# Six-layer cross network on one core: first group half turned by DMA, another order of the last jobs, the last layer regrouped

## The chip, the cores and the metric

The kernel runs on one core of a Trainium2 chip. The metric is the device time of one execution in microseconds (us): the median of 13 runs is 494.12 (491.48 to 496.78). Lower is better.

The engines have names as in the profile: PE is the matrix engine, PEld its weight loads, DVE the vector engine, ACT the scalar engine, POOL the one for odd work, SP the one that here only issues DMAs. ACT issues some DMAs too; on either engine the issue is an instruction of its queue, taken in order with the rest.

## The reference

A cross network of six layers over 16384 rows of 416 features in bf16:

```
x = x0                                   # [16384, 416]
for l in range(6):
    proj = einsum('bd,de->be', x, ws[l]) + bs[l]
    x = x0 * proj + x
return x
```

Each layer is one 416 x 416 matrix product, a bias, a product with the input x0 and a sum with the layer's own input.

## The kernel before

**Tiling.** The rows are cut into 8 groups of 2048 (`GC`), each into 4 chunks of 512 (`CH`, index j). Inside the kernel x is kept turned: features on the 128 partitions, rows along the free axis. The 416 features are three tiles of 128 (index t or i) and a rest of 32; the rest of all four chunks is packed on one 128-partition tile (`x3`, 32 partitions a chunk). Group g and layer l make a job (g, l); a job is three output tiles and a tail (the 32 last outputs). `full` (L399) issues the twelve 128x128 matmuls of a tile, `rows32` (L412) the four that take the 32 rest rows, `tails` (L422) the tails of several jobs. `evacuate` (L347) empties a tile: ACT adds the bias on the way out of PSUM (L364), DVE multiplies by x0 (L373) and adds x (L378). A tail goes the same way (L391, L393, L395).

**Order.** `order` (L217) lists the 48 jobs by hand along diagonals, so that two jobs of one group have others between them, but for the first two and the last two. `items` turns it into tiles and batches of tails; tiles go in pairs, the first with the rest rows last (FR), the second with the rest rows first (RF), singles are F1. At the end one tile of job (6, 5) is put between two of (7, 4) (L565). `Program` keeps one queue for each engine in program order and works out the semaphore waits from what each instruction reads and writes; DVE's adds are held back behind the next product (`hold`, `release`). An instruction that waits holds everything behind it on its engine.

**Front.** Group 0 comes in natural layout, a chunk at a time (`load_nat`, L459, on SP). PE turns it: 28 small matmuls on an identity first (L480), then for each chunk twelve transposes (L494) and four for the rest columns (L499), emptied by ACT (L504, twice a chunk) and DVE (L507, L510). The biases are turned likewise (L639 to L648). `load_w3` (L282) issues four small loads of a layer's last 32 weight rows; layers 0 and 1 go on ACT's queue. Every other group but the last is turned by DMA (`load_group`, L294): three transposes of 2048 x 128, one of the last 128 columns into `Tb`, and from there four copies of 32 partitions, each waiting for `Tb` (L305).

**End.** When a group's last layer is done, `output` (L531) turns it back by DMA into `ost` on SP's queue: tile 0, tile 1, four small transposes of the rest (L543), tile 2 (L535), then, after all have landed, one store (L550). Group 7's last layer is computed with rows on the partitions instead (from L759): `nat_full` (L716) and `nat_rows` (L727, L732) for each of four row sets kk, `to_rows` turns x by PE (L691, L698) and ACT and DVE copy it out (L708, L711), `nat_mul` (L744, L746; the very last one directly from PSUM, L741), `nat_add` (L751), `nat_store` (L756).

Of the kernel before, what the change touches and what calls it, by code (L numbers as in the profile page):

```python
# [3 lines left out]
P = 128  # L4
CH = 512
T32 = 32
# [192 lines left out]
def bass_standalone__cross_network_dcn__recsys_kernel(  # L199
# [19 lines left out]
             (2, 4), (3, 3), (4, 1), (5, 0)]  # L219
    order += [(NG - 1 - g, L - 1 - l) for g, l in reversed(order)]  # L220
    assert len(set(order)) == NG * L
    cuts = [1, 2, 3, 4, 4, 4, 4, 4, 4, 4, 4, 4, 3, 2]
# [14 lines left out]
    bs_sb = nc.alloc_sbuf_tensor("bs_sb", [P, D], BF16)  # L237
    brow = nc.alloc_sbuf_tensor("brow", [P, D], BF16)
    ones = nc.alloc_sbuf_tensor("ones", [P, P], BF16)
    x0s = [nc.alloc_sbuf_tensor(f"x0_{s}", [P, XW + CH], BF16) for s in range(NX0)]  # L240
# [105 lines left out]

    def evacuate(g, l, i, banks, js, step):  # L347

# [6 lines left out]
        src, stok = x_src(g, l)  # L355
        so = xset[(g, l + 1)]
        a = js[0]
        while a <= js[-1]:
# [100 lines left out]
    def load_nat(j, k0, k1):  # L459
        add("sp", lambda h: h.dma_start(x0n[:, j, k0:k1, :], perm(g0, j)[:, k0:k1, :]),  # L460
            writes=[("nat", j, k) for k in range(k0, k1)], lane=f"nat{j}{k0}", batch=0)

    add("act", lambda h: h.dma_start(bs_sb[0:L, :], bs[:, :]), writes=["bs_sb"], lane="bs", batch=0)
    load_nat(0, 0, 2)
    load_nat(0, 2, KK)
    load_wm(0, "sp")
    load_w3(0, "act")
    make_wbd(0)
    for j in range(1, NJ):
        load_nat(j, 0, KK)  # L470
    load_wm(1, "sp")
    load_w3(1, "act")
    load_group(1)
# [4 lines left out]

    for _ in range(28):
        add("pe", lambda h: h.matmul(psum[:, 7 * CH:7 * CH + P], ident[:, :], ident[:, :], start=True, stop=True),  # L480
            reads=["ident"], writes=[("ps", 7)])

    def psum_t(b):
        return psum[:, b * CH:(b + 1) * CH].bitcast(BF16)

    def transposed_chunk(j):
        ba, bb = (0, 1) if j % 2 == 0 else (2, 3)
        s = slot(0)
        for t in range(NT + 1):
            b, o = (ba, t * CH) if t < 2 else (bb, (t - 2) * CH)  # L490
            for k in range(KK):
                c = slice(o + k * P, o + (k + 1) * P)
                if t < NT:
                    add("pe", lambda h, t=t, k=k, b=b, c=c: h.transpose(  # L494
                        psum_t(b)[:, c], x0n[:, j, k, t * P:(t + 1) * P], ident[:, :]),
                        reads=[("nat", j, k), x0_tok(nat, 0, 0), "ident"], writes=[("ps", b)])
                else:
                    q = slice(j * T32, (j + 1) * T32)
                    add("pe", lambda h, k=k, b=b, c=c, q=q: h.matmul(  # L499
                        psum_t(b)[q, c], x0n[:, j, k, NT * P:D], ident[:, :], is_transpose=True,  # L500
                        tile_position=(0, j * T32)),
                        reads=[("nat", j, k), x0_tok(nat, 0, 0), "ident"], writes=[("ps", b)])
        for t in range(2):
            add("act", lambda h, t=t: h.activation(  # L504
                x0s[s][:, cols(t, j)], psum_t(ba)[:, t * CH:(t + 1) * CH], ACT_F.Copy),
                reads=[("ps", ba)], writes=[x0_tok(s, t, j)])
        add("dve", lambda h: h.tensor_copy(x0s[s][:, cols(2, j)], psum_t(bb)[:, 0:CH]),  # L507
            reads=[("ps", bb)], writes=[x0_tok(s, 2, j)])
        q = slice(j * T32, (j + 1) * T32)
        add("dve", lambda h: h.tensor_copy(x0s[s][q, XW:XW + CH], psum_t(bb)[q, CH:2 * CH]),  # L510
            reads=[("ps", bb)], writes=[("x03q", s, j)])


# [17 lines left out]
    def output(g):  # L531
# [9 lines left out]
        for j in range(NJ):  # L541
# [5 lines left out]
        rows = out[g * GC:(g + 1) * GC, :]  # L547
        pat = "(j p k) f -> p j k f" if g == 0 else "(j k p) f -> p j k f"
        kw = dict(j=NJ, k=KK)
        add("sp", lambda h: h.dma_start(  # L550
            rows.rearrange(pat, **kw), ost[:, :, :].rearrange("p (j k) f -> p j k f", j=NJ)),
            reads=[("ost", t) for t in range(NT)] + [("ost", NT, j) for j in range(NJ)],
            writes=[("out", g)], lane="out", batch=g)
        free_x.append(s)
# [3 lines left out]
    where = {(b[min(1, len(b) - 1)], 0): b for b in batches[:-1]}  # L558
    where[((LAST - 1, L - 1), 1)] = batches[-1]
    for jb in order[:-1]:  # L560
        for i in range(NT):
            items.append(("tile", jb, i))
            if (jb, i) in where:
                items.append(("tails", where[(jb, i)]))
    late = items.index(("tile", (LAST - 1, L - 1), NT - 1))  # L565
    items.insert(len(items) - 2, items.pop(late))

# [29 lines left out]

    fine_after = {(0, 0), (LAST, L - 2)}
    k = 0
    open_rf = None  # L600
    tiles_done = {}

    def finish_tile(g, l):
        tiles_done[(g, l)] = tiles_done.get((g, l), 0) + 1
        if tiles_done[(g, l)] == NT:
            done_with(g, l)
# [15 lines left out]

    first_tile = True
    for n, it in enumerate(items):
# [4 lines left out]
        if (g, l) not in started:  # L629
            start_job(g, l)  # L630
        fine = (g, l) in fine_after
        step = 1 if fine and i == NT - 1 else 2
        if mode[n] in ("FR", "F1"):
            if first_tile:
                first_tile = False
                transposed_chunk(0)
                bt = 7
                for t in range(NT):
                    add("pe", lambda h, t=t: h.transpose(  # L639
                        psum_t(bt)[:, t * 8:t * 8 + L], bs_sb[0:L, t * P:(t + 1) * P], ident[0:L, 0:L]),  # L640
                        reads=["bs_sb", "ident"], writes=[("ps", bt)])
                for j in range(NJ):
                    q = slice(j * T32, (j + 1) * T32)
                    add("pe", lambda h, j=j, q=q: h.matmul(
                        psum_t(bt)[q, NT * 8:NT * 8 + L], bs_sb[0:L, NT * P:D], ident[0:L, 0:L],
                        is_transpose=True, tile_position=(0, j * T32)),
                        reads=["bs_sb", "ident"], writes=[("ps", bt)])
                add("act", lambda h: h.activation(  # L648
                    bias[:, :, :], psum_t(bt)[:, 0:32].rearrange("p (t l) -> p t l", l=8)[:, :, 0:L], ACT_F.Copy),
                    reads=[("ps", bt)], writes=["bias"])  # L650
                banks = [4, 5, 6, 7]
                for j in range(1, NJ):
                    transposed_chunk(j)
                    full(g, l, i, banks, True, True, chunks=[j - 1])
                full(g, l, i, banks, True, True, chunks=[NJ - 1])
            else:
                banks = job_banks()
                full(g, l, i, banks, True, fine and i == NT - 1)
            rows32(g, l, i, banks, False)
            evacuate(g, l, i, banks, list(range(NJ)), step)  # L660
        else:
            banks = job_banks()
            rows32(g, l, i, banks, True)
            if step == 1:
                full(g, l, i, banks, False, True,
                     lambda j, g=g, l=l, i=i, banks=banks: evacuate(g, l, i, banks, [j], 1))
            else:
                full(g, l, i, banks, False, False)
                evacuate(g, l, i, banks, list(range(NJ)), step)
        finish_tile(g, l)  # L670


# [86 lines left out]
    bka, bkb = take(NJ), take(NJ)  # L759
    for j in range(NJ):  # L760
        nat_full(0, j, bka[j], True)
    nat_rows(0, bka, False)
    for j in range(NJ):
        nat_mul(0, j, bka[j])
    nat_rows(1, bkb, True)
    for j in range(NJ):
        nat_full(1, j, bkb[j], False)
        nat_mul(1, j, bkb[j])
    to_rows(0, bka)
    to_rows(1, bkb)  # L770
    nat_rows(2, bka, True)
    for kk in range(2):
        for j in range(NJ):
            nat_add(kk, j)
        nat_store(kk, 0, NJ, f"out7_{kk}")
    for j in range(NJ):
        nat_full(2, j, bka[j], False)
        nat_mul(2, j, bka[j])
        if j:
            nat_add(2, j - 1)  # L780
    nat_add(2, NJ - 1)
    nat_store(2, 0, NJ, "out7_2")
    nat_rows(3, bkb, True)
    for j in range(NJ):
        nat_full(3, j, bkb[j], False)
        nat_mul(3, j, bkb[j])
        if j:
            nat_add(3, j - 1)
        if j == 2:
            nat_store(3, 0, 2, "out7_3")  # L790
    nat_add(3, NJ - 1)
    nat_store(3, 2, NJ, "out7_4", "act")

# [29 lines left out]
```

## Time and profile before

| | us |
|---|---|
| median of 13 runs | 494.12 |
| the profiled execution | 491.52 |
| its span, first to last instruction | 489.7 |
| PE, DVE, ACT busy | 472.9, 405.7, 343.3 |
| DMA: 47.65 MB, mean | 97 GB/s |

The span is what the instructions cover; the 1.8 us to the execution's time lie around it. The page's second part cuts the span into 40 equal slices of 12.2 us, each a digit for the busy tenths of an engine. A line of a timeline gives start, length, engine, line of the kernel, operation, what is written and read, how many were merged, and in brackets how long the engine had been idle before it and what ended that. An engine's name with q behind it is its queue: a DMA issue or a wait, in which the engine does no work. The length of an issue is not that of the transfer; the landing is a separate event of the trace. A line of the view by stretches gives the stretch, its length, the busy time of PE, PEld, DVE, ACT and POOL, the granted clock of PE as a share, the DMA share and GB/s. Lengths of matmuls overlap; the distance from start to start tells the rate.

### The profile page before, as it was taken

How to read it: one execution, taken by the hardware profiler on the slowest of the kernel's cores; microseconds unless marked ns; L12 is line 12 of the kernel's file. 1: busy time of each engine (PE TensorE's matmuls, PEld its weight loads, DVE VectorE, ACT ScalarE, POOL GpSimd, SP SyncE). 2: the span in 40 equal slices, each digit the busy share in tenths (PEclk: the TensorE clock that was granted, in tenths of full speed). 3: DMA queues.
4: the chain of work that ended last, by engine and by line, in shares of the span. 5: the costliest groups of instructions: out<-in, count | busy, mean ns of one | idle time of the engine just before them, and what ended most of it. 6: DMA issues, size and time to landing. Idle time of an engine off the chain costs nothing.

```text
span 489.7 us, 8048 instructions
## 1 busy us (share of the span) xinstructions
PE 472.9 (97%) x3197; PEld 202.7 (41%) x3251; DVE 405.7 (83%) x710; ACT 343.3 (70%) x372; POOL 11.4 (2%) x37
## 2 busy tenths in 40 slices
PE   7999999999999999999999999999999999999985
PEld 6343444444444444444444444444444444344443
DVE  1778888888888888888888888888888888888877
ACT  3676777677677677767677767767767776677765
POOL 2022200000000000000000000000000000000000
PEclk9999999999999999999999999999999999999998
DMA  8795972000001387269316962570000236045656
GB/s 248 142 188 133 178 142 53 0 1 0 2 1 37 62 227 139 50 114 225 77 20 121 229 93 40 112 269 1 1 1 1 44 55 183 8 80 136 146 137 194
DMA packets 127689, 47.65 MB, mean 97 GB/s; under 512 B 107674, under 2 KB 126244, under 8 KB 127652
## 3 DMA queue, kind: packets, MB, share of 16 engines
q1 hardware_dynamic: 126984, 46.71, 42.9%
q8 instruction: 25, 0.41, 0.3%
q10 hardware_dynamic: 668, 0.43, 0.3%
q14 instruction: 12, 0.10, 0.1%
HBM read 5.97 MB, written 13.63 MB: 40 GB/s over the span
## 4 chain that ended last, share of the span: by engine, by line
PE 90%; DVE 4%; ACT 2%; issue 2%; DMA 1%; SPq 0%; DVEq 0%
PE ps L405 73%; PE ps L417 8%; PE ps L430 5%; ACT tw L364 2%; PE ps L435 2%; DMA x<-in_x_dram 1%; DVE x L378 1%; PE ps L716 1%; DVE x L751 1%; DVE tw L373 1%; PE ps L691 1%; PE ps L494 0%; DVE x L746 0%; ACT ts L391 0%; PE ps L499 0%
## 5 line engine op out<-in xcount | busy, mean ns | idle before, releaser
L364 ACT ACTIVATE tw<-ps,bias 128x1024 bf16<-128x1024 f32 (+1 forms) x296 | 300.6, 1070 | 129.8 <-PE ps L417 107.7
L405 PE MATMUL ps<-x,wm 128*128 128x512 bf16 x1638 | 372.6, 379 | 6.5 <-issue 3.7
L373 DVE TENSOR_TENSOR tw<-tw,x 128x1024 bf16<-128x1024 bf16 (+1 forms) x286 | 194.1, 683 | 68.4 <-ACT tw L364 68.1
L405 PEld LDWEIGHTS ps<-x,wm 128*128 128x128 bf16 x1692 | 158.8, 98 | 215.7 <-issue 28.2
L378 DVE TENSOR_TENSOR x<-tw,x 128x1024 bf16<-128x1024 bf16 (+1 forms) x286 | 182.1, 678 | 0.0
L417 PE MATMUL ps<-x,w 32*128 32x512 bf16 x564 | 44.5, 380 | 0.3 <-DVE x L395 0.3
L430 PE MATMUL ps<-x,wm 128*32 128x512 bf16 x564 | 38.7, 380 | 0.0
L391 ACT ACTIVATE ts<-ps,bias 128x512 bf16<-128x512 f32 x47 | 28.7, 699 | 0.0
L417 PEld LDWEIGHTS ps<-x,w 32*128 32x128 bf16 x564 | 9.0, 92 | 33.5 <-issue 32.4
L430 PEld LDWEIGHTS ps<-x,wm 128*32 128x32 bf16 x564 | 13.8, 96 | 15.5 <-issue 3.2
L395 DVE TENSOR_TENSOR x<-ts,x 128x512 bf16<-128x512 bf16 x47 | 18.7, 422 | 0.0
L393 DVE TENSOR_TENSOR ts<-ts,x 128x512 bf16<-128x512 bf16 x47 | 18.7, 421 | 0.0
L435 PE MATMUL ps<-x,wbd 128*32 128x512 bf16 x188 | 18.3, 379 | 0.0
L716 PE MATMUL ps<-wm,x 128*128 128x416 bf16 x48 | 9.7, 343 | 1.7 <-DVE x L378 1.7
L291 POOL COPY wbd<-w 32x32 bf16<-32x32 bf16 x24 | 9.3, 386 | 39.8 <-DMA w<-in_ws_dram 38.6
L507 DVE COPY x<-ps 128x512 bf16<-128x512 bf16 x4 | 1.7, 424 | 10.1 <-PE ps L499 10.1
L744 ACT ACTIVATE x<-ps 128x416 bf16<-128x416 f32 x15 | 6.8, 536 | 3.1 <-PE ps L732 2.4
L716 PEld LDWEIGHTS ps<-wm,x 128*128 128x128 bf16 x48 | 4.9, 116 | 6.2 <-DVE x L378 2.8
L435 PEld LDWEIGHTS ps<-x,wbd 128*32 128x32 bf16 x188 | 5.0, 97 | 5.1
L746 DVE TENSOR_TENSOR x<-x,x 128x416 bf16<-128x416 bf16 x15 | 5.4, 373 | 1.9 <-ACT x L744 1.7
L504 ACT ACT_TABLE_LOAD x1 | 1.3, 1283 | 6.3 <-issue 6.3
L504 ACT ACTIVATE x<-ps 128x512 bf16<-128x512 bf16 x8 | 4.3, 602 | 1.2 <-PE ps L494 1.2
(32 smaller groups left out, 42.7 us busy)
## 6 DMA issues: line engine op xcount, KB each, us to landing
out_dram<-ost SPq DMA_DIRECT2D x7, 1664.0 KB, 7.4
x<-in_x_dram SPq DMA_DIRECT2D x7, 416.0 KB, 6.4
wm<-in_ws_dram SPq DMA_DIRECT2D x6, 312.0 KB, 3.4
out_dram<-x SPq DMA_DIRECT2D x3, 416.0 KB, 2.9
x<-Tb SPq DMA_DIRECT2D x28, 32.0 KB, 1.8
ost<-x SPq DMA_TRANSPOSE x49, 2.4
x<-in_x_dram SPq DMA_DIRECT2D x2, 208.0 KB, 2.7
w<-in_ws_dram SPq DMA_DIRECT2D x16, 26.0 KB, 2.2
```

The lines of the kernel that those rows point to most:

```text
L291: add("pool", lambda h, q=q: h.tensor_copy(wbd[l][q, q], w3[l][q, NT * P:D]), reads=[("w3", l, j)], writes=[("wbd", l)])
L364: add("act", lambda h, a=a, w=w, b0=b0: h.activation(tw[r][:, a * CH:(a + w) * CH], psum[:, b0 * CH:(b0 + w) * CH], ACT_F.Identity, bias=b ...
L373: add("dve", lambda h, a=a, e=e: h.tensor_tensor(tw[r][:, a * CH:e * CH], tw[r][:, a * CH:e * CH], x0s[s0][:, i * GC + a * CH:i * GC + e * ...
L378: add("dve", lambda h, a=a, e=e: h.tensor_tensor(xs[so][:, i * GC + a * CH:i * GC + e * CH], tw[r][:, a * CH:e * CH], src(i, a, e), ALU.ad ...
L391: add("act", lambda h: h.activation(ts[r][:, :], bank(b), ACT_F.Identity, bias=bias[:, 3, l:l + 1], scale=1.0), reads=[("ps", b), "bias"], ...
L393: add("dve", lambda h: h.tensor_tensor(ts[r][:, :], ts[r][:, :], x0s[s0][:, XW:XW + CH], ALU.mult), reads=[("ts", r)] + x03_toks(s0), writ ...
L395: add("dve", lambda h: h.tensor_tensor(x3s[so][:, :], ts[r][:, :], src, ALU.add), reads=[("ts", r)] + stok, writes=[("x3", so)], hold=True)
L405: add("pe", lambda h, t=t, j=j: h.matmul(bank(banks[j]), wm[l][:, t, ecols], src(t, j, j + 1), start=(first and t == 0), stop=(not first a ...
L417: add("pe", lambda h, q=q, j=j: h.matmul(bank(banks[j]), w3[l][q, ecols], src[q, :], start=first, stop=not first, tile_position=(j * T32, 0)),
L430: add("pe", lambda h, t=t, j=j, src=src, l=l, b=b: h.matmul(bank(b, j * T32, (j + 1) * T32), wm[l][:, t, NT * P:D], src(t, j, j + 1), star ...
L435: add("pe", lambda h, j=j, s3=s3, l=l, b=b: h.matmul(bank(b, j * T32, (j + 1) * T32), wbd[l][:, j * T32:(j + 1) * T32], s3, start=False, s ...
L716: add("pe", lambda h, t=t: h.matmul(bank(b, n=D), xcol(t, j, kk), wm[l][:, t, :], start=(first and t == 0), stop=(not first and t == NT - 1)),
```

## The change

- Of group 0 only chunks 0 and 1 are loaded in natural layout and turned by PE. Chunks 2 and 3 are turned by DMA: SP issues a transpose of 1024 rows into half of `Tb`, three more into x0, and ACT's queue gets the two copies from `Tb` to x0.
- ACT runs a small activation first (on a tile that DVE clears); layer 1's small weights are issued by SP; 14 small matmuls stand ahead of the transposes instead of 28; chunk 0 is turned in two halves.
- Job (0, 0) is written out (`first_job`): its tile 0 and 1 by chunks, half of tile 0 emptied by DVE alone (`vector` in `evacuate`), tile 2 chunk by chunk, the job's tail last.
- The last jobs run as (5,5), (7,3), (6,4), (7,4), (6,5), (7,5); no tile is moved among them, and the last tails stand after tile 0 of (7, 4).
- The last layer turns two row sets, computes one, turns the other two, computes three; products, adds and stores follow each row set; the last store holds one chunk instead of two.
- Group 0's store is two DMAs.

```diff
--- before.py
+++ after.py
@@ -218,6 +218,7 @@
              (0, 4), (1, 3), (2, 2), (3, 1), (0, 5), (1, 4), (2, 3), (3, 2), (4, 0), (1, 5),
              (2, 4), (3, 3), (4, 1), (5, 0)]
     order += [(NG - 1 - g, L - 1 - l) for g, l in reversed(order)]
+    order[-6:] = [(5, 5), (7, 3), (6, 4), (7, 4), (6, 5), (7, 5)]
     assert len(set(order)) == NG * L
     cuts = [1, 2, 3, 4, 4, 4, 4, 4, 4, 4, 4, 4, 3, 2]
     batches = []
@@ -236,6 +237,7 @@
     bias = nc.alloc_sbuf_tensor("bias", [P, 4, L], FP32)
     bs_sb = nc.alloc_sbuf_tensor("bs_sb", [P, D], BF16)
     brow = nc.alloc_sbuf_tensor("brow", [P, D], BF16)
+    warm = nc.alloc_sbuf_tensor("warm", [P, 8], FP32)
     ones = nc.alloc_sbuf_tensor("ones", [P, P], BF16)
     x0s = [nc.alloc_sbuf_tensor(f"x0_{s}", [P, XW + CH], BF16) for s in range(NX0)]
     xs = [nc.alloc_sbuf_tensor(f"x_{s}", [P, XW], BF16) for s in range(NXS)]
@@ -344,7 +346,7 @@
             if 4 < g + NX0 <= LAST:
                 load_group(g + NX0)
 
-    def evacuate(g, l, i, banks, js, step):
+    def evacuate(g, l, i, banks, js, step, vector=()):
 
         s0 = slot(g)
         r = tw_n[0] % NTW
@@ -354,6 +356,17 @@
             r = (tw_n[0] - 1) % NTW
         src, stok = x_src(g, l)
         so = xset[(g, l + 1)]
+        for a in vector:
+            o = slice(a * CH, (a + 1) * CH)
+            add("dve", lambda h, a=a, o=o: h.scalar_tensor_tensor(
+                out=tw[r][:, o], in0=bank(banks[a]), scalar=bias[:, i, l:l + 1],
+                in1=x0s[s0][:, i * GC + a * CH:i * GC + (a + 1) * CH], op0=ALU.add, op1=ALU.mult),
+                reads=[("ps", banks[a]), "bias", x0_tok(s0, i, a)], writes=[("tw", r, a)])
+        for a in vector:
+            o = slice(a * CH, (a + 1) * CH)
+            add("dve", lambda h, a=a, o=o: h.tensor_tensor(
+                xs[so][:, i * GC + a * CH:i * GC + (a + 1) * CH], tw[r][:, o], src(i, a, a + 1), ALU.add),
+                reads=[("tw", r, a), stok(i, a)], writes=[("x", so, i, a)])
         a = js[0]
         while a <= js[-1]:
             if step > 1 and a % 2 == 0 and a + 1 <= js[-1] and banks[a + 1] == banks[a] + 1:
@@ -460,23 +473,35 @@
         add("sp", lambda h: h.dma_start(x0n[:, j, k0:k1, :], perm(g0, j)[:, k0:k1, :]),
             writes=[("nat", j, k) for k in range(k0, k1)], lane=f"nat{j}{k0}", batch=0)
 
+    add("dve", lambda h: h.memset(warm[:, :], 0.0), writes=["warm"])
+    add("act", lambda h: h.activation(warm[:, :], warm[:, :], ACT_F.Identity, bias=0.0, scale=1.0),
+        reads=["warm"], writes=["warm"])
     add("act", lambda h: h.dma_start(bs_sb[0:L, :], bs[:, :]), writes=["bs_sb"], lane="bs", batch=0)
     load_nat(0, 0, 2)
     load_nat(0, 2, KK)
     load_wm(0, "sp")
+    load_nat(1, 0, KK)
     load_w3(0, "act")
     make_wbd(0)
-    for j in range(1, NJ):
-        load_nat(j, 0, KK)
+    half = slice(2 * CH, GC)
+    add("sp", lambda h: h.dma_start_transpose(Tb[:, half], g0[half, D - P:D]), writes=["Tb"], lane="Tb", batch=0)
+    for t in range(NT):
+        add("sp", lambda h, t=t: h.dma_start_transpose(
+            x0s[0][:, t * GC + 2 * CH:(t + 1) * GC], g0[half, t * P:(t + 1) * P]),
+            writes=[x0_tok(0, t, j) for j in (2, 3)], lane=f"x0_00{t}", batch=0)
+    for j in (2, 3):
+        q = slice(j * T32, (j + 1) * T32)
+        add("act", lambda h, q=q, j=j: h.dma_start(x0s[0][q, XW:XW + CH], Tb[P - T32:P, j * CH:(j + 1) * CH]),
+            reads=["Tb"], writes=[("x03q", 0, j)], lane="x03_00", batch=0)
     load_wm(1, "sp")
-    load_w3(1, "act")
+    load_w3(1, "sp")
     load_group(1)
     load_wm(2, "sp")
     load_w3(2, "sp")
     make_wbd(1)
     make_wbd(2)
 
-    for _ in range(28):
+    for _ in range(14):
         add("pe", lambda h: h.matmul(psum[:, 7 * CH:7 * CH + P], ident[:, :], ident[:, :], start=True, stop=True),
             reads=["ident"], writes=[("ps", 7)])
 
@@ -486,20 +511,22 @@
     def transposed_chunk(j):
         ba, bb = (0, 1) if j % 2 == 0 else (2, 3)
         s = slot(0)
-        for t in range(NT + 1):
+        seq = [(t, k) for t in range(NT) for k in range(KK)]
+        if j == 0:
+            seq = [(t, k) for k2 in (0, 2) for t in range(NT) for k in (k2, k2 + 1)]
+        for t, k in seq + [(NT, k) for k in range(KK)]:
             b, o = (ba, t * CH) if t < 2 else (bb, (t - 2) * CH)
...
+            c = slice(o + k * P, o + (k + 1) * P)
...
@@ -510,6 +537,41 @@
         add("dve", lambda h: h.tensor_copy(x0s[s][q, XW:XW + CH], psum_t(bb)[q, CH:2 * CH]),
             reads=[("ps", bb)], writes=[("x03q", s, j)])
 
+    def first_job():
+
+        g, l = 0, 0
+        start_job(g, l)
+        transposed_chunk(0)
...
+        ba, bb = [4, 5, 6, 7], [0, 1, 2, 3]
+        full(g, l, 0, ba, True, True, chunks=[0])
+        transposed_chunk(1)
+        full(g, l, 0, ba, True, True, chunks=[1])
+        full(g, l, 1, bb, True, True, chunks=[0, 1])
+        full(g, l, 0, ba, True, True, chunks=[2, 3])
+        rows32(g, l, 0, ba, False)
+        evacuate(g, l, 0, ba, [0, 1], 2, vector=[2, 3])
+        full(g, l, 1, bb, True, True, chunks=[2, 3])
+        rows32(g, l, 1, bb, False)
+        rows32(g, l, 2, ba, True)
+        evacuate(g, l, 1, bb, list(range(NJ)), 2)
+        full(g, l, 2, ba, False, True, lambda j: evacuate(g, l, 2, ba, [j], 1))
+        finish_tile(g, l, NT)
+        tails([(g, l)])
+
 
     def job_banks():
         return take(NJ)
@@ -545,25 +607,27 @@
                 reads=[("x3", s3)], writes=[("ost", NT, j)], lane="ot", batch=g)
         turn(2)
         rows = out[g * GC:(g + 1) * GC, :]
-        pat = "(j p k) f -> p j k f" if g == 0 else "(j k p) f -> p j k f"
-        kw = dict(j=NJ, k=KK)
-        add("sp", lambda h: h.dma_start(
-            rows.rearrange(pat, **kw), ost[:, :, :].rearrange("p (j k) f -> p j k f", j=NJ)),
-            reads=[("ost", t) for t in range(NT)] + [("ost", NT, j) for j in range(NJ)],
-            writes=[("out", g)], lane="out", batch=g)
+        o = ost[:, :, :].rearrange("p (j k) f -> p j k f", j=NJ)
+        parts = [("(j k p) f -> p j k f", 0, NJ)]
+        if g == 0:
+            parts = [("(j p k) f -> p j k f", 0, 2), ("(j k p) f -> p j k f", 2, NJ)]
+        for pat, j0, j1 in parts:
+            add("sp", lambda h, pat=pat, j0=j0, j1=j1: h.dma_start(
+                rows[j0 * CH:j1 * CH, :].rearrange(pat, j=j1 - j0, k=KK), o[:, j0:j1, :, :]),
+                reads=[("ost", t) for t in range(NT)] + [("ost", NT, j) for j in range(NJ)],
+                writes=[("out", g, j0)], lane="out", batch=g)
...
     items = []
     where = {(b[min(1, len(b) - 1)], 0): b for b in batches[:-1]}
-    where[((LAST - 1, L - 1), 1)] = batches[-1]
-    for jb in order[:-1]:
+    where[((LAST, L - 2), 0)] = batches[-1]
+    del where[((0, 0), 0)]
+    for jb in order[1:-1]:
         for i in range(NT):
             items.append(("tile", jb, i))
             if (jb, i) in where:
                 items.append(("tails", where[(jb, i)]))
-    late = items.index(("tile", (LAST - 1, L - 1), NT - 1))
-    items.insert(len(items) - 2, items.pop(late))
 
 
     single = 0
...
-    first_tile = True
+    first_job()
     for n, it in enumerate(items):
         if it[0] == "tails":
             tails(it[1])
@@ -628,45 +689,16 @@
         _, (g, l), i = it
...
         if mode[n] in ("FR", "F1"):
...
-                full(g, l, i, banks, True, fine and i == NT - 1)
+            banks = job_banks()
+            full(g, l, i, banks, True, False)
             rows32(g, l, i, banks, False)
-            evacuate(g, l, i, banks, list(range(NJ)), step)
+            evacuate(g, l, i, banks, list(range(NJ)), 2)
         else:
             banks = job_banks()
             rows32(g, l, i, banks, True)
-            if step == 1:
-                full(g, l, i, banks, False, True,
-                     lambda j, g=g, l=l, i=i, banks=banks: evacuate(g, l, i, banks, [j], 1))
-            else:
-                full(g, l, i, banks, False, False)
-                evacuate(g, l, i, banks, list(range(NJ)), step)
+            full(g, l, i, banks, False, False)
+            evacuate(g, l, i, banks, list(range(NJ)), 2)
         finish_tile(g, l)
 
 
@@ -757,39 +789,31 @@
             reads=[("on", j, kk) for j in range(j0, j1)], writes=[("out7", kk, j0)], lane=lane, batch=0)
 
     bka, bkb = take(NJ), take(NJ)
-    for j in range(NJ):
-        nat_full(0, j, bka[j], True)
-    nat_rows(0, bka, False)
-    for j in range(NJ):
-        nat_mul(0, j, bka[j])
-    nat_rows(1, bkb, True)
-    for j in range(NJ):
-        nat_full(1, j, bkb[j], False)
-        nat_mul(1, j, bkb[j])
+    last = KK - 1
+
+    def layer_rows(kk, bks):
+        nat_rows(kk, bks, True)
+        for j in range(NJ):
+            nat_full(kk, j, bks[j], False)
+            nat_mul(kk, j, bks[j])
+            if j:
+                nat_add(kk, j - 1)
+            if kk == last and j == 2:
+                nat_store(kk, 0, 2, "out7_3")
+            if kk == last and j == 3:
+                nat_store(kk, 2, 3, "out7_4")
+        nat_add(kk, NJ - 1)
+        if kk < last:
+            nat_store(kk, 0, NJ, f"out7_{kk}")
+        else:
+            nat_store(kk, NJ - 1, NJ, "out7_5", "act")
+
     to_rows(0, bka)
-    to_rows(1, bkb)
-    nat_rows(2, bka, True)
-    for kk in range(2):
-        for j in range(NJ):
-            nat_add(kk, j)
-        nat_store(kk, 0, NJ, f"out7_{kk}")
-    for j in range(NJ):
-        nat_full(2, j, bka[j], False)
-        nat_mul(2, j, bka[j])
-        if j:
-            nat_add(2, j - 1)
-    nat_add(2, NJ - 1)
-    nat_store(2, 0, NJ, "out7_2")
-    nat_rows(3, bkb, True)
-    for j in range(NJ):
-        nat_full(3, j, bkb[j], False)
-        nat_mul(3, j, bkb[j])
-        if j:
-            nat_add(3, j - 1)
-        if j == 2:
-            nat_store(3, 0, 2, "out7_3")
-    nat_add(3, NJ - 1)
-    nat_store(3, 2, NJ, "out7_4", "act")
+    layer_rows(0, bkb)
+    to_rows(1, bka)
+    layer_rows(1, bkb)
+    layer_rows(2, bka)
+    layer_rows(3, bkb)
 
     pr.emit()
 
```

## The prediction

> **What bounds the kernel now.** I read the page's busy row first, then the chain that ended last in order of time, then the timeline of the two ends, the SP queue among it.
>
> ```profile
> PE 472.9 (97%) x3197; PEld 202.7 (41%) x3251; DVE 405.7 (83%) x710; ACT 343.3 (70%) x372; POOL 11.4 (2%) x37
> PE   7999999999999999999999999999999999999985
> ```
>
> TensorE is busy 97% and in tenths of 9 from slice 2 to slice 38; only the first and the last two slices show room. The middle needs no further reading: what the change moves at either end comes through one for one. The front, in the timeline:
>
> ```profile
> 1.79 3.17 PE L480 MATMUL ps<-ident 128*128 128x128 bf16 x28 [1.79 <-POOL ident L449]
> 6.30 1.28 ACT L504 ACT_TABLE_LOAD   x1 [6.30 <-issue]
> 7.59 1.09 ACT L504 ACTIVATE x<-ps 128x512 bf16<-128x512 bf16 x2
> ...
> 16.81 2.35 SPq L301 DMA_TRANSPOSE Tb<-in_x_dram  x1
> 21.33 2.50 SPq L305 DMA_DIRECT2D x<-Tb  x4
> ...
> 24.06 0.39 PE L405 MATMUL ps<-x,wm 128*128 128x512 bf16 x1 [0.28 <-DVE x L378]
> 25.39 0.61 PE L417 MATMUL ps<-x,w 32*128 32x512 bf16 x8
> ```
>
> ACT issues eight weight DMAs until 6.27, loads its table until 7.58, then empties chunk 0. PE waits for the vector engine until 24.7; from the L417 at 25.39 (job (0,1)) it runs on. SP waits from 19.16 to 21.33 for Tb to land before L305: an engine that issues such a DMA stands until its source is there. The end:
>
> ```profile
> 462.78 5.00 SPq L543 DMA_TRANSPOSE ost<-x  x4
> ...
> 468.14 0.54 PE L716 MATMUL ps<-wm,x 128*128 128x416 bf16 x2
> ...
> 468.96 1.96 SPq L535 DMA_TRANSPOSE ost<-x  x1
> ...
> 470.40 2.23 PE L716 MATMUL ps<-wm,x 128*128 128x416 bf16 x10 [1.73 <-DVE x L378]
> ...
> 473.25 0.37 SPq L550 DMA_DIRECT2D out_dram<-ost  x1
> ...
> 481.19 5.22 SPq L756 DMA_DIRECT2D out_dram<-x  x4
> ...
> 485.93 0.59 DVE L741 TENSOR_TENSOR x<-ps,x 128x416 bf16<-128x416 f32 x1
> ```
>
> Call T = 468.14 the start of the last layer. PE stalls 1.73 there on x(7,5), and ends at 484.42; DVE, behind with its adds, takes the last product only at 485.93. Group 6's store leaves at T+5.1, in time. The span ends at T+21.5.
>
> **Front, step by step.** Removed: the PE transposes of chunks 2 and 3 (2 x 16 at 0.056, 1.8) with four ACT and four DVE copies; 14 of the warm-up matmuls (14 x 0.107 = 1.5); the table load leaves the path (1.28). Chunk 0 lies in PSUM by about 5.3 instead of 6.4. But the two copies Tb to x0 are now in ACT's queue ahead of L504, and ACT waits in order for Tb.
>
> When does Tb land? SP's first four issues are unchanged; chunk 1, the last before Tb, lands at 7.8 (the chain shows 2.13 + 5.66). In the old trace the first 2048-row transpose lands 3.0 after the plain load ahead of it (14.47 after 11.43), later ones 2.1 to 2.5 apart; half the rows give 1.4 to 2.1. So Tb lands at 9.2 to 9.9; I take 9.6. Then ACT issues two DMAs: 0.33 to 0.52 each while SP issued plain loads, 0.81 and 1.26 for the two beside SP's transposes, which it is beside now. I take 0.8 each. ACT begins chunk 0 at **A = 11.3** (bounds 9.9 to 12.4), against 7.59. Queued behind it: the bias copy, chunk 1's copies, every first-job evacuation; PE waits for them, and DVE for PE.
>
> From A: two ACT copies and the last matmul to A+1.6; eight transposes, two copies, the remaining matmul of chunk 1 to A+3.8; twelve matmuls at 0.216 and four row matmuls to A+6.7 = R, the end of tile 0's rows. The halves that come by DMA land in steps of 1.2 after Tb, by 13.4, before PE wants them at A+5.1. After R the vector engine sets the pace: two PSUM products (L741 goes at 0.50 for 416 columns, so 0.62 each), two 512 adds at 0.335, six 1024 operations at 0.60, eight 512 ones, and the tail's two, which now come last: 1.24 + 0.67 + 3.6 + 2.7 + 0.7 = 8.9, with 0.45 for start and gaps 9.35. The rows of job (0,1), which read that tail, start at R+9.35 = A+16.05. Against 25.39: A - 9.34 = **+2.0** (+0.6 to +3.1).
>
> The clock adds to it:
>
> ```profile
> 484.50:487.00 2.50, 0.00 (x0) 0.00 (x0) 2.50 (x9) 0.00 (x0) 0.00 (x0) 1.00 0.61 176
> 487.00:489.70 2.70, 0.00 (x0) 0.00 (x0) 0.08 (x1) 0.00 (x0) 0.00 (x0) 0.52 0.47 163
> ```
>
> The granted clock (the column after POOL) falls to a half 2.7 after the last matmul. At the start matmuls lie 107 ns apart until 5.7, 56 after: 3.9 of work to full speed. Now PE idles from about 6 to A+0.6, six microseconds, so the 18 matmuls and 16 transposes before R begin at half speed. All of it slow would be +4.0; no drop, 0. With 3.9 of work to recover, chunk 1 is half done by then and R comes 0.9 later; I take **+1.0**, nearest that row.
>
> [...]
>
> [...]
>
> At nothing: layer 1's small weights move from ACT's to SP's queue and, with four half transposes, stand ahead of group 1's loads. [...] The biases and layer 0's small weights are issued some 2 us later, behind the table load: the former are wanted only after chunk 0, the latter at R. The split store of group 0 and the vector engine's memset lie beside PE's work. In the new order the tail of (6,5) reads what (6,4) tile 2 leaves: such a tile's x was ready 3.6 after its matmuls (468.93 after 465.3), and job (7,4)'s tile 0 and tail keep PE busy for some 4.2; if not, 0.5 is lost.
>
> **End, step by step.** Gains: job (6,5) now lies between (7,4) and (7,5), so the 1.73 stall goes. PE's last layer is two turns of 1.6 and four times 2.8, T+14.5. DVE has eight operations per 2.8 at 0.285, 2.3, so it keeps up; last product, two adds: T+16.1, against T+18.9. By compute alone the end gains **2.85**.
>
> What is late next is SP. Tile 1 of (6,5) stands where tile 2 stood in the old order, so x is ready at T+0.8 (468.93). Then in SP's order: turn 1, 1.95; four small transposes, 5.0 (they took 5.0 to 5.8 in every group); turn 2, 1.95; landing 2.3: group 6's store leaves at T+12.1 instead of T+5.1. All last-layer stores but one are queued behind it. It lands 7.4 after issue (median; 6.6 to 8.6); its 1.7 MB went at 325 GB/s, and 1.6 MB more follow: 4.85. The end is T + 12.1 + 7.4 + 4.85 + 0.45 = T+24.8, against T+21.5: **+3.3** (2.5 to 4.4). The smaller last store on ACT's queue saves nothing behind that.
>
> Sum: 2.0 + 1.0 + 3.3 = +6.3. The profiled execution took 491.5 (span 489.7): 497.8 for its like. It lies 2.6 under the median of 494.12, so I state 494.1 + 6.3 = **500.4**.
>
> **Rivals.** First, ACT's wait is cheap: Tb lands by 9, the clock holds, the front is even; the end still drains late: +3.3, 497.4. For it: the table load is gone; against: chunk 1's own landing at 7.8.
> Second, the stores are no bound: 1.6 MB spread over idle DMA time, so -2.85 at the end, +3.0 at the front: about 494.3, no change. Against it: SP's queue is in order.
> Third, faster: the same removed stall and backlog, worth 2.85, with a front of +0.6 or less: 491.9 or below. It decides if group 6's store leaves before about T+6 (then 3.4 MB are out by T+18.7); that takes the four small transposes done before tile 1's turn, and the code puts them behind it.
>
> **Numbers.** Forecast 0.62, first rival 0.16, second 0.12, third 0.10. The measurement tells 0.3%, 1.5 us, from no change. So slower 0.78, within 0.12, faster 0.10. The forecast's bounds alone are +3.1 to +11.5, the upper end only if every cost is at its worst; with the first rival and a part of the second I give 495.5 to 503.5.
>
> **What would show it.** ACT's first L504 near 11.3, with its copies' issue just before, waiting on Tb. Matmuls at 0.43 apart after it. Job (0,1)'s first L417 near 28.4. No DVE wait at the last layer; the store of group 6 12 after its start; the SP queue waiting for stores when all engines are done. I am wrong if ACT starts by 9, or if SP's small transposes run before the tiles are ready.

## The result

The changed kernel takes 498.41 us (median of 11, 497.41 to 499.59). The kernel before, run beside it, takes 493.28 (median of 48, 490.75 to 498.03). The ratio is 1.0103, 95% interval 1.0079 to 1.0128: slower by 5.1 us, clear of the noise. The forecast was 500.4, or 6.3 slower, in a range of 495.5 to 503.5.

| profiled execution | before | after |
|---|---|---|
| time; span | 491.52; 489.7 | 499.07; 497.3 |
| ACT begins chunk 0 (A of the prediction) | 7.59 | 10.52 |
| first row matmul of job (0,1) | 25.39 | 28.67 |
| start of the last layer (T) | 468.14 | 471.42 |
| group 6's store leaves, after T | 5.11 | 13.57 |
| DVE done, after T | 18.94 | 16.49 |
| end, after T | 21.55 | 25.85 |

The spans differ by 7.6: 3.28 up to T and 4.30 behind it. From the first row matmul of job (0,1) to T both traces need 442.75, so all of the loss lies at the two ends. The page of the changed kernel, to be read beside that of before:

```profile
PE 471.3 (95%) x3152; PEld 200.8 (40%) x3205; DVE 404.0 (81%) x705; ACT 340.5 (68%) x366; POOL 11.5 (2%) x37
PE   4999999999999999999999999999999999999990
```

PE is busy 1.6 us less, and is idle in half of the first slice and in all of the last. The front, from the timelines of ACT and PE:

```profile
2.33 0.91 ACTq L286 DMA_DIRECT2D w<-in_ws_dram  x2
9.21 1.27 ACTq L494 DMA_DIRECT2D x<-Tb  x2
10.52 1.08 ACT L531 ACTIVATE x<-ps 128x512 bf16<-128x512 bf16 x2 [8.29 <-issue]
...
11.18 1.52 PE L418 MATMUL ps<-x,wm 128*128 128x512 bf16 x3 [5.43 <-ACT x L531]
12.49 1.49 PE L521 MATMUL ps<-ident,x 128*128 128x128 bf16 x12
...
14.85 3.95 PE L418 MATMUL ps<-x,wm 128*128 128x512 bf16 x14 [0.33 <-ACT x L531]
18.73 0.39 PE L430 MATMUL ps<-x,w 32*128 32x512 bf16 x4
...
28.67 0.61 PE L430 MATMUL ps<-x,w 32*128 32x512 bf16 x8 [0.41 <-DVE x L408]
```

ACT issues its last weight load by 3.24 and does nothing until 9.21, when it issues the two copies: that gap is the wait for Tb. Only then does it empty chunk 0, which PE had turned by 5.5. PE stands 5.43 for it. The twelve transposes of chunk 1 take 1.49 here; in the old kernel they took 0.84, at full clock:

```profile
7.84 0.84 PE L494 MATMUL ps<-ident,x 128*128 128x128 bf16 x12 [1.16 <-DMA x<-in_x_dram]
```

Twelve such transposes take 1.49 in end_only, too, at 10.65, where the granted clock is 0.50: PE works at half clock here. The chain of waits names the cause of the late start in one line:

```profile
2.67 6.52 DMA Tb<-in_x_dram
```

It is 21.7% of the first 30 us. The end, first the SP queue from the timeline, then the last instructions of the chain:

```profile
469.77 4.55 SPq L597 DMA_TRANSPOSE ost<-x  x2
474.36 6.25 SPq L605 DMA_TRANSPOSE ost<-x  x4
480.65 1.88 SPq L597 DMA_TRANSPOSE ost<-x  x1
484.99 0.37 SPq L615 DMA_DIRECT2D out_dram<-ost  x1
485.41 7.31 SPq L788 DMA_DIRECT2D out_dram<-x  x5
```

```profile
486.84 0.50 DVE x L773
487.34 0.28 DVE x L783
487.63 0.28 DVEq L174
```

DVE is done at 487.9. The stores behind group 6's are issued from 485.41 on, and the last lands at 496.7. One of them is issued by ACT at 487.94 and needs 5.42 to land (2.09 in the old kernel), so it is not SP's queue alone that holds them: they land behind group 6's 1.7 MB. The stall at the last layer's start is gone: PE goes from T to its end in 14.66 instead of 16.28.

### The profile page after: what moved, and what is told of

It reads as the page before. It is cut to its first block, busy times and chain, and to the rows that moved or that the text cites. A ratio compares the mean times of both kernels' runs of the same rounds, so it can differ in the third digit from the quotient of the medians.

```text
span 497.3 us, 7944 instructions
## 1 busy us (share of the span) xinstructions
PE 471.3 (95%) x3152; PEld 200.8 (40%) x3205; DVE 404.0 (81%) x705; ACT 340.5 (68%) x366; POOL 11.5 (2%) x37
## 4 chain that ended last, share of the span: by engine, by line
PE 90%; DVE 2%; ACT 2%; issue 2%; DMA 1%; SPq 0%; ACTq 0%; DVEq 0%
PE ps L418 73%; PE ps L430 8%; PE ps L443 5%; PE ps L448 2%; PE ps L748 1%; ACT tw L377 1%; DMA Tb<-in_x_dram 1%; DVE x L391 1%; DVE tw L386 1%; ACT x L531 0%; PE ps L723 0%; SPq L473 0%; ACTq L494 0%; ACT ts L404 0%; PE ps L759 0%
## 5 line engine op out<-in xcount | busy, mean ns | idle before, releaser
L443 PEld LDWEIGHTS ps<-x,wm 128*32 128x32 bf16 x564 | 13.8, 96 | 15.7 <-issue 2.9
L534 DVE COPY x<-ps 128x512 bf16<-128x512 bf16 x2 | 0.8, 424 | 12.9 <-PE ps L526 12.9
L531 ACT ACTIVATE x<-ps 128x512 bf16<-128x512 bf16 x4 | 2.2, 594 | 10.2 <-issue 8.3
L778 DVE TENSOR_TENSOR x<-x,x 128x416 bf16<-128x416 bf16 x15 | 5.5, 372 | 0.5 <-ACT x L776 0.4
L783 DVE TENSOR_TENSOR x<-x,x 128x416 bf16<-128x416 bf16 x16 | 5.6, 371 | 0.0
```

Of the source, the lines that this page charges most:

```text
L443: add("pe", lambda h, t=t, j=j, src=src, l=l, b=b: h.matmul(bank(b, j * T32, (j + 1) * T32), wm[l][:, t, NT * P:D], src(t, j, j + 1), star ...
```

## The experiments

Theory: the loss has two causes that add. In front ACT, which has to empty chunk 0, stands in order for Tb. At the end group 6's store leaves 8.5 us later after T, because SP takes two tiles and four small transposes between the last layer's start and it, and the last layer's stores wait behind it. Rivals: one of the two alone; transposes that are late whoever waits for them; the bytes of the end; the half clock.

All runs in one table; times of the trace from each run's profiled execution. The runs come from three chips, each with the kernel before beside them (medians 493.18, 492.43 and 493.05), so across chips the ratios compare better than the medians.

| kernel | median | ratio to before (95%) | A | first row matmul of (0,1) | T | end after T |
|---|---|---|---|---|---|---|
| front_only | 494.25 | 1.0020 (0.9988 to 1.0052) | 10.04 | 27.69 | 470.44 | 21.53 |
| end_only | 496.76 | 1.0050 (1.0020 to 1.0080) | 8.18 | 27.40 | 470.15 | 25.74 |
| copies_on_sp | 494.05 | 1.0016 (0.9985 to 1.0047) | 4.60 | 23.46 | 466.61 | 25.86 |
| small_first | 493.94 | 1.0013 (0.9981 to 1.0045) | 11.05 | 29.20 | 471.96 | 21.39 |
| no_store6 | 491.88 | 0.9988 (0.9972 to 1.0004) | 10.35 | 28.59 | 471.34 | 18.81 |
| order_only_end | 498.65 | 1.0115 (1.0086 to 1.0144) | 10.31 | 27.98 | 470.73 | 25.93 |
| pe_filler | 497.11 | 1.0103 (1.0087 to 1.0120) | 10.54 | 28.06 | 470.81 | 25.17 |
| pe_filler_long | 498.26 | 1.0101 (1.0075 to 1.0127) | 10.15 | 26.77 | 469.52 | 26.30 |
| old_filler | 492.27 | 1.0000 (0.9974 to 1.0026) | 8.97 | 26.33 | 469.08 | 21.56 |
| both_mended | 490.17 | 0.9960 (0.9944 to 0.9977) | 4.64 | 23.72 | 466.48 | 21.31 |
| mended_front_old_order | 490.73 | 0.9945 (0.9926 to 0.9964) | 4.73 | 24.05 | 467.57 | 20.76 |
| first_rows_first | 489.75 | 0.9928 (0.9902 to 0.9954) | 4.81 | 24.48 | 467.43 | 20.82 |

**front_only**: the new front, old order and old last layer.

```diff
-    order[-6:] = [(5, 5), (7, 3), (6, 4), (7, 4), (6, 5), (7, 5)]
-    where[((LAST, L - 2), 0)] = batches[-1]
+    where[((LAST - 1, L - 1), 1)] = batches[-1]
+    late = items.index(("tile", (LAST - 1, L - 1), NT - 1))
+    items.insert(len(items) - 2, items.pop(late))
...
```

> The new front with the old job order and the old last layer. Theory (the loss has two parts, a front where ACT stands for Tb and an end where group 6's store leaves late): the first row matmul of job (0,1) at about 28.7 instead of 25.4, the last layer as of old (stall of 1.7, end 21.5 after its start), time +1.5 to +3.3 on the kernel before. Rival (the end alone costs, the front's delay is hidden later): within 0.5 of the kernel before.

By the trace it is the theory, if a little less of it: the row matmul comes at 27.69, 2.3 later than in the old profile (28.7 was expected), T is 2.3 later, the end 21.5 behind T. By the times it lies between the two: 494.25 against 493.18, and the interval takes in 1. So the time alone does not show the front's cost here. The next run shows one reason why the times can give less than two profiles do.

**end_only**: the old front with the new order and the new last layer (the other half of the change).

> The old front with the new job order and the new last layer. Theory: group 6's store leaves some 13 after the last layer's start, all engines are done 16 to 17 after it, the end comes 25 to 26 after it, time +2.5 to +4.4 on the kernel before; with front_only it sums to the whole change. Rival (the end is as good as its removed stall, the loss is the front's): -2.9 to 0.

As the theory has it: DVE done at T+16.5, group 6's store at T+13.2, the end at T+25.7; the time is 2.5 to 3.6 up, by the ratio or by the medians. Together with front_only's loss that makes 4.7 by the medians or 0.7% by the ratios, against 5.1 and 1.0% for the whole change. The two parts add, as far as intervals of some 0.3% to either side can tell. But its front, unchanged in code, reaches the row matmul at 27.40 and not at 25.39. The view by stretches of this run:

```profile
5.00:9.40 4.40, 2.90 (x39) 2.32 (x38) 0.74 (x2) 2.50 (x5) 0.98 (x5) 1.00 0.99 332
9.40:12.80 3.40, 3.07 (x21) 2.11 (x21) 0.93 (x3) 1.99 (x4) 0.03 (x1) 0.50 1.32 233
12.80:16.00 3.20, 3.20 (x29) 1.68 (x27) 1.61 (x4) 1.11 (x3) 1.01 (x5) 0.99 1.21 174
```

The granted clock is 0.50 from 9.4 to 12.8. In the profile of before it is 1.00 there:

```profile
9.40:12.80 3.40, 3.40 (x39) 2.37 (x38) 1.59 (x5) 2.23 (x5) 0.81 (x4) 1.00 1.18 221
```

The old front has a short wait of PE for chunk 1 (1.16 in the old profile, 1.50 here), after which the clock fell in this execution, at 9.43. Of the 2.0 that this front is late, 0.45 is chunk 1's later landing; the rest, 1.56, comes while the clock is at a half. Among 35 executions of the kernel before on this chip, 17 show a mean granted clock of 0.996 or more and have a median of 491.7; the other 18 have 495.0. The mean is a rough sign, because the profile counts the time before an execution's first clock record as full clock (in the changed kernel's all up to 16.38), and it does not say where the clock was low. Still, the profiled execution of before, 491.52, lies with the faster half, and a new front compared with the median of both halves loses less than the two profiles say.

**copies_on_sp**: the two copies from Tb are issued by SP.

```diff
-        add("act", lambda h, q=q, j=j: h.dma_start(x0s[0][q, XW:XW + CH], ...
+        add("sp", lambda h, q=q, j=j: h.dma_start(x0s[0][q, XW:XW + CH], ...
```

> The changed kernel, but the two copies from Tb to x0 are issued by SP behind its four half transposes instead of by ACT. Theory (ACT's wait for Tb holds the front): ACT empties chunk 0 near 5.5, job (0,1)'s first row matmul comes at 23.5 to 25.5, time 3 to 5 below the changed kernel. Rival (the DMA transposes themselves are late, whoever issues the copies): the halves land at 13.5 either way and the first row matmul stays at 28 to 29, time within 0.7 of the changed kernel.

The theory holds: ACT begins at 4.60, the row matmul comes at 23.46, 5.2 before that of the changed kernel, and the time falls by 4.4 (by 0.9% in the ratio). ACT's timeline, to be read against the one above:

```profile
2.33 0.91 ACTq L286 DMA_DIRECT2D w<-in_ws_dram  x2
4.60 1.09 ACT L531 ACTIVATE x<-ps 128x512 bf16<-128x512 bf16 x2 [2.35 <-PE ps L521]
5.66 0.19 ACT L556 ACTIVATE bias<-ps 128x24 f32<-128x24 bf16 x1
8.31 1.09 ACT L531 ACTIVATE x<-ps 128x512 bf16<-128x512 bf16 x2 [2.46 <-PE ps L521]
```

It now waits for PE, not for a DMA. PE no longer stands long, and the clock stays up from 5.82 on, so the 5.2 hold the half clock as well as the wait. The row matmul also comes 1.9 sooner than in the old profile: the other parts of the new front, which were not taken out one by one, cost nothing together. The halves land at 12.5 and the copies at 12.9, not later than by ACT (13.5, 13.8). With the front this early the cover of the next loads runs out: group 1's last piece lands at 29.77, and the row matmuls that want it start at 29.90, 0.4 late; the last layer starts 4.8 sooner than in the changed kernel.

**small_first**: for group 6, the small transposes ahead of the tiles.

```diff
-        turn(0)
-        turn(1)
+        if g < LAST - 1:
+            turn(0)
+            turn(1)
         for j in range(NJ):
...
+        if g == LAST - 1:
+            turn(0)
+            turn(1)
         turn(2)
```

> The changed kernel, but for group 6 the four small transposes stand ahead of those of the tiles in SP's queue. Theory (SP's order makes the store late, and the last layer's stores queue behind it): the store leaves 7.5 to 8.5 after the last layer's start instead of 13.6, the end comes 20 to 21.5 after it instead of 25.9, time 4 to 5.5 below the changed kernel. Rival (the bytes of the last 25 us are too many whenever they start, or DVE sets the end): less than 1.5 below.

The theory holds again: same bytes, same engines, only SP's order. The SP queue:

```profile
470.31 7.72 SPq L597 DMA_TRANSPOSE ost<-x  x3
480.84 0.37 SPq L619 DMA_DIRECT2D out_dram<-ost  x1
481.26 7.89 SPq L792 DMA_DIRECT2D out_dram<-x  x5
```

The store leaves at T+8.9 (7.5 to 8.5 was expected), the end comes at T+21.4, the time falls by 4.5 (0.9% in the ratio).

**no_store6**: group 6's store left out.

```diff
-        for pat, j0, j1 in parts:
+        for pat, j0, j1 in (parts if g < LAST - 1 else []):
```

> The changed kernel without group 6's store (its 2048 rows of the output are not written). Theory (the last layer's stores wait behind it): all stores landed 18.3 to 18.9 after the last layer's start, which is when DVE's last sum allows it, the end at 19 instead of 25.9, time 6 to 7 below the changed kernel. Rival (the chain through DVE and the last layer's own stores is late anyway): less than 3 below.

The last store lands at T+18.33, the end comes at T+18.81, 7.0 earlier; the time is 6.5 lower by the medians, 1.15% or 5.7 by the ratios. So with nothing queued ahead the end is set by compute and the last layer's own stores, and the store of group 6 costs all that lies behind T+18.81.

**order_only_end**: the new order with the old last layer.

> The changed kernel with the old last layer (new front, new job order). Theory (the order makes group 6's store late, the regrouped last layer is innocent): store 13 to 14 after the last layer's start, end 25 to 26.5 after it, time within 0.7 of the changed kernel. Rival (the regrouped stores are at fault): 2 or more below.

Store at T+13.6, end at T+25.9, the time that of the changed kernel within the intervals: it is the order that costs, not the regrouped layer. DVE is done at T+16.74 here, against 16.49 with the regrouped layer: once the stall is gone the old grouping is hardly behind.

**pe_filler**: matmuls on the identity while PE waits for ACT; 60 of them, then 95.

```diff
+        for _ in range(60):
+            add("pe", lambda h: h.matmul(psum[:, 6 * CH:6 * CH + P], ident[:, :], ident[:, :], start=True, stop=True),
+                reads=["ident"], writes=[("ps", 6)])
         ba, bb = [4, 5, 6, 7], [0, 1, 2, 3]
```

> The changed kernel with 60 idle matmuls on the identity (into a bank that is not yet in use) between the bias turn and chunk 0's first matmul, so that PE does not stand while ACT waits for Tb. Theory (half clock is a part of the front's cost): matmuls before the first row matmul lie 0.22 apart instead of 0.43, that one comes at 16.5 to 17.5 instead of 18.7, time 1 to 2 below the changed kernel. Rival (waits for ACT and DVE hide the half clock): less than 0.4 below.

Missed: they ended at 9.0, PE stood 2.6, and the clock was at a half from 11.94 to 15.36. The row matmuls of tile 0 came 7.58 after A, against 8.21 in the changed kernel.

**pe_filler_long**

> As pe_filler, but 95 idle matmuls, so that less than 1 us stays idle before chunk 0's matmuls (with 60 PE still stood 2.6 us and the clock fell at 11.9). Theory (half clock is a part of the front's cost): the clock stays at 1.0, the first row matmul comes at 16.8 to 17.6, time 1 to 2 below the changed kernel. Rival (waits hide the half clock): less than 0.4 below.

PE, in the view by stretches and the timeline of this run:

```profile
5.00:9.00 4.00, 4.00 (x66) 3.77 (x65) 0.74 (x2) 0.00 (x0) 0.25 (x2) 1.00 1.20 251
9.00:13.00 4.00, 4.00 (x63) 3.46 (x60) 0.00 (x0) 1.61 (x4) 0.76 (x4) 1.00 1.45 141
```

```profile
11.27 0.81 PE L418 MATMUL ps<-x,wm 128*128 128x512 bf16 x3
11.91 0.83 PE L521 MATMUL ps<-ident,x 128*128 128x128 bf16 x12
...
16.83 0.40 PE L430 MATMUL ps<-x,w 32*128 32x512 bf16 x4
```

The transposes are back at 0.83, and tile 0's row matmuls come 6.68 after A, 1.5 sooner than in the changed kernel's profile; the last layer starts 1.9 sooner, 0.4 of it from an earlier A. The time, expected 1 to 2 lower, does not show it: ratio 1.0101 against 1.0103, each with an interval of a quarter per cent to either side. So these two profiles show that the half clock costs some 1.5 in the profiled front; what it costs in the median of executions is open, between nothing and that.

**old_filler**: the old kernel with 16 such matmuls over its short wait.

> The kernel before with 16 idle matmuls between the bias turn and chunk 1, where PE stands 1.1 us. Theory (the old front, too, loses its clock in a part of its executions: end_only's profile has it at a half from 9.4 to 12.8 and its front is 2 late, the old profile has not): fewer of them, time 0.5 to 1.5 below the kernel before and less spread. Rival (the spread of the kernel before is of another kind): within 0.4, the same spread.

The time is that of before. Its twelve runs reach from 491.5 to 495.0, the 26 of before on that chip from 491.1 to 498.0; three of twelve have a mean granted clock below 0.995, against 13 of the 26. So the clock seems to fall less often, but the median does not gain. In its profile the clock is full from 5.72 on (the mean is 1.00), and the front is still 0.9 later than in that of before (row matmul at 26.33): ACT's eight weight DMAs took 6.30 to issue instead of 4.92, and A came at 8.97 instead of 7.59. The faster half's advantage is thus not shown to be the clock's alone.

**both_mended**: copies_on_sp and small_first together.

> The changed kernel with the copies from Tb on SP and group 6's small transposes first. If the two causes add: the last layer starts at 466.6, the end comes 21.4 after it, span 488, median 4 to 4.5 below each of the two alone and 3 to 4.5 below the kernel before. Rival (the gains overlap): no better than the better of the two, some 494.

In the trace the gains add: T at 466.5, the end 21.3 behind it, a span of 487.8, all within some 0.2 of what was expected. In time they come to less: 490.17 is 3.8 to 3.9 below each of the two alone, on another chip, and 2.3 below the kernel before beside it (3 to 4.5 was expected). It still beats the kernel before (0.9960, interval 0.9944 to 0.9977) and the changed one.

**mended_front_old_order**: copies_on_sp, with the old order and the regrouped last layer.

> The changed kernel with the copies from Tb on SP, the old order of the last jobs (stall before the last layer back) and the regrouped last layer. Theory (the regrouping alone is a gain of what DVE was behind, the store is in time): end 20 to 20.7 after the last layer's start against 21.5 of old, time 0.3 to 1.3 below both_mended. Rival (without the order the regrouping gains nothing): end at 21.5 or later, time equal to both_mended or above.

The end comes at T+20.76, with the stall back (1.97 on x(7,5)), in the expected direction by 0.8 against the old order's 21.55. T itself is 1.1 later than in both_mended, 0.77 of it another wait for group 1's last piece. The times do not part the two (490.73 and 490.17 on two chips, ratios 0.9945 and 0.9960 with overlapping intervals): no difference is shown between the new order with the small transposes first and the old order.

**first_rows_first**: both_mended, with group 6's store behind the first of the last layer.

```diff
...
+        if g == LAST - 1:
+            later.append(store)
...
             nat_store(kk, 0, NJ, f"out7_{kk}")
+            if kk == 0:
+                later.pop()()
```

> both_mended with group 6's store issued behind the first store of the last layer, which is ready before it. Theory (the end is the time to drain 3.4 MB after group 6's store leaves, so 0.4 MB moved ahead of it is saved): end 20.0 to 20.4 after the last layer's start instead of 21.3, time 0.8 to 1.4 below both_mended. Rival (the issue of the first store holds the larger one back as long): within 0.4.

The end moves from T+21.31 to T+20.82, half of what was expected. The last layer's first store, whose rows are only summed by then, leaves at T+7.5, 1.3 ahead of group 6's, and lands in 3.8; group 6's then takes 7.6 instead of 6.7. It has the lowest median and ratio of all (0.9928, 489.75 against 493.05 for the kernel before beside it), but its interval, 0.9902 to 0.9954, overlaps that of both_mended, so the times do not decide between theory and rival.

## Why the prediction was right, point by point

- **Tb holds ACT.** Right. Tb landed at 9.19 (forecast 9.2 to 9.9, taken 9.6), the two issues took 0.63 and 0.61 (taken 0.8 each): A at 10.52 instead of 11.3. In copies_on_sp, which changes nothing but who waits for Tb, the row matmul comes 5.2 sooner in the trace, and the time falls by 4.4.
- **From A to the row matmuls.** R, the end of tile 0's row matmuls, was put at A+6.7 at full clock and A+7.7 with the half clock. In pe_filler_long, at full clock, it comes at A+7.08, in the changed kernel at A+8.60. From R (19.12) to the row matmuls of job (0,1), 9.35 was forecast for DVE's work and 9.55 measured.
- **The half clock.** Taken as 1.0; 1.5 in the profile of the changed kernel, 0.9 to 1.0 in those of pe_filler, front_only and order_only_end (7.58, 7.71 and 7.72 from A to the start of the row matmuls, against 6.68 at full clock). The mechanism was only half right. In front_only the clock rises at 4.65 and falls again at 8.06, as forecast. In the changed kernel's own profile all matmuls up to 16.1 are slow and the first record of a full clock is at 16.38, so it had not risen at all, and 5.2 passed from PE's start at 11.18 until it rose, where 3.9 had been taken. (The view by stretches prints 1.00 for the time before the first record; the 1.49 for twelve transposes tells the clock: 1.49 in end_only at a granted 0.50, 0.84 in before at 7.84, behind its first record of a full clock at 5.81.)
- **Front in all.** +3.0 forecast, +3.28 measured between the profiles. That they are so close is in part luck: A came 0.8 sooner, the way from A to R took 0.9 longer and the rest 0.2 longer than forecast. The middle, forecast to pass it on unchanged, passes it on to the hundredth.
- **Group 1's loads.** Layer 1's small weights and the half transposes ahead of them were put at nothing, and they cost nothing: the last piece landed at 29.78 (25.07 in before), and PE did not wait for it. The cover was thin: with the copies on SP the piece lands at 29.77 and PE waits 0.4 for it.
- **The end by compute.** DVE done at T+16.1 forecast, 16.49 measured; no_store6 ends at T+18.81 with nothing queued ahead.
- **The late store.** The mechanism was right, as small_first, no_store6 and order_only_end show; the size was off: the store leaves at T+13.57 where T+12.1 was forecast. The term is the four small transposes: 6.25 instead of the 5.0 that was taken. The store landed in 6.6 (7.4 taken), the rest followed in 5.1 (4.85): end at T+25.85 instead of 24.8, +4.3 instead of +3.3.
- **The sum.** The two profiled executions are 7.6 apart (forecast 6.3), the medians 5.1. The weak step is the one that carried the profile's difference over to the median: it took the 2.6 by which the profiled execution lay below the median for a shift that both kernels have. It is not one. The old kernel's profiled execution lies 1.8 below its median of 48, the changed kernel's 0.7 above its own. So two errors partly cancel: front and end were forecast 1.3 too small together, and the difference of profiles is 2.4 larger than that of medians. That the forecast's difference is only 1.2 too large is luck to this extent; the other 0.8 of the 2.0 between 500.4 and 498.41 is the median of 13 that it started from. Why the old kernel's executions spread so stays open: end_only shows a half clock in its front as one cause, old_filler a late ACT as another, and neither was shown for the faster and the slower half as a whole.
- **The rivals.** The cheap wait is out: A is at 10.52, the front 3.28 late and at half clock. That the stores are no bound is out, by small_first and no_store6. The faster case needed group 6's store by about T+6 and a front of +0.6 or less, and the change has neither; both_mended, with the store at T+8.8 and a front 1.7 sooner than the old one, is faster by 0.4%.

## What to carry to other kernels

A DMA that depends on another DMA should not be issued by an engine that has work to do soon. Here it waited in order and everything behind it waited too: ACT began at 10.52 instead of 4.60, 5.9 us later, for two small copies. When the last big store is moved later, count what is queued behind it and how many bytes have to drain after it leaves. Here a stall of 1.73 on the compute side was removed, and the end came 4.3 later all the same. Before two profiles are subtracted, look where the profiled executions lie among their runs: the difference of two executions is not that of two medians.

## What the runs showed of the hardware

- In each of these profiles the records of the granted clock lie multiples of 3.41 us apart: 4.65, 8.06 and 14.89 in front_only (3.41 and twice 3.41), 6.01, 9.43 and 12.84 in end_only, 5.81 and 487.09 in before (141 times 3.413), 16.38 and 490.83 in the changed kernel (139 times 3.413). Where this grid lies in the span differs between executions: with the same front, the first rise is at 4.65 in front_only, 4.95 in order_only_end and 16.38 in the changed kernel, no two of them a multiple of 3.41 apart.
- PE was not idle all through the 3.41 before a fall. In pe_filler it worked some 0.8 of the 3.41 before the fall at 11.94, in end_only some 1.9 of the 3.42 before the fall at 9.43; in before it worked 2.1 of the 3.41 from 5.81 and the clock stayed.
- In before the clock stayed up over PE work that was nearly all transposes: of those 2.1 all but 0.05 are transposes, and from 9.40 to 12.80 the granted clock is 1.00. Ahead of a rise the profiles differ in more than one way. In before the 3.41 up to the first record of a full clock, at 5.81, hold 3.41 of PE work, 2.6 of it the small matmuls issued ahead of the transposes; in the changed kernel the stretch from 2.72 to 6.14 (16.38 less three and four times 3.41) holds 3.0, only 0.7 of it such matmuls, and no rise follows until 16.38. What makes the difference is not shown. With the same 14 of these matmuls ahead the clock rose at 4.65 in front_only and at 16.38 in the changed kernel.
- Four SBUF-to-SBUF transposes of 32 x 512 kept SP for 5.00 in before (462.78, 1.25 each), where no other DMA was in flight, and for 6.25 in the changed kernel (474.36). They move little, 32 KB each, but what was queued behind them on SP was late by that much.
